# Sines of integer phases: contiguous reads, strided writes, and another order of multiples, sines and the upper half's sum

## The chip, the cores and the metric

The kernel runs on one core of a Trainium2 chip. The metric is the device time of one execution in microseconds (us), the median of several runs. The core's engines work in parallel, each through its own queue in program order: TensorE (PE, matmuls; PEld is its weight load), VectorE (DVE), ScalarE (ACT, activations), GpSimd (POOL) and SyncE (SP, which issues most DMAs). An instruction that waits holds back all that stand behind it in its engine's queue.

## The reference, cut to what matters

Two layers, each a state-space convolution and a gated feed-forward block, over 2048 tokens of 512 channels, in fp32:

```
x = x + ssm(layernorm(x));  x = x + ffn(layernorm(x))     # twice
ssm:  logdA = dt * (A_re + i A_im)          # 512 channels x 128 states
      P[d,n,l] = exp(logdA[d,n] * l)        # l = 0..2047
      K[d,l]   = Re sum_n C[d,n] P[d,n,l] dt B[d,n]
      y = causal convolution of u with K (by FFT) + u * Dskip
ffn:  (silu(x @ w_gate) * (x @ w_up)) @ w_down
```

The change lies in how the kernel makes K: for every channel and state it needs powers exp(logdA * l), whose phase is l * dt * A_im. The phase is kept as an integer, a fraction of a turn in 32 bits, so that a multiple of it is an integer sum that wraps around by itself.

## The kernel before, in words

The 128 states lie on the 128 partitions. The 512 channels are done in 8 chunks of 64 (DC = 64). A power l = 64 b + a is split into a table over a (`re`, `im`, 64 channels x 65 entries, made from exponentials, sines and cosines of multiples) and a table over b (`g`, made by doubling). For each chunk `lags` (L486) multiplies the two on TensorE, 128 small matmuls, into K; K goes by a copy (`spread_in`, L497) and DMAs into the order in which `spectra` (L534) transforms it.

The steps that the change and the prediction touch:

- `turn_units` (L362) turns dt * A_im into integers of a turn, `th` (one step) and `th32` (32 steps): two products on VectorE (L370), a conversion to integers on ScalarE (L371), a subtraction and two conversions on VectorE (L372, L374). Its scratch is `ft`. It runs for the channels 0 to 127 at the start, and for 128 to 255 and 256 to 511 later (L942, L951, L952).
- `gen_turns` (L376), VectorE: five small multiples for the doubling, into `xz` (L380), and sixteen multiples of `th32` into the scratch `tu` (L382, L386), which has the order partition, multiple m, channel d.
- `gen_trig` (L391), ScalarE, in three steps. First the small ones (L395 and one round of L399 to L401 on `xz`). Then for the lower half, m = 0 to 15: absolute value into `re` (L399), sine into `im` (L400), cosine in place in `re` (L401). Then the same for the upper half. `re` and `im` have the order channel, multiple, with 65 entries (260 bytes) per channel. L399 and L400 read `tu` through a transposed view, so they read at a stride of 256 bytes and write in runs of 16.
- `gen_upper` (L404), VectorE: adds the sixteenth multiple to all sixteen, in place in `tu` (L407). It must come after the lower half's sines have read `tu`, and before the upper half's.
- `gen_exp` (L409), ScalarE: five Exps into `mz`, twenty Exps into columns of `re` (L419), two squares (L431). `upper` (L423): a square into `mu` (L425).
- `gen_e` (L434) and `gen_g` (L451), VectorE: the products that finish `re` and `im` (L440 to L448) and the doubling of `g` (L455 to L483; `take(gg, n)` does n steps of it). The last doubling ends with a DMA that adds (L473).
- `gen_w` (L174), VectorE: the product of B, C and dt. `norm_early` (L278) normalizes the first 512 tokens; `direct` (L283) transforms them on TensorE (L289), and ScalarE copies the result out (L292).
- `norms` (L304) loads pieces of the feed-forward weights; ScalarE squares them (L323), TensorE sums the squares (L326), VectorE takes the largest (L329).

ScalarE holds one set of function tables at a time. Exp and Sin are in different sets, and a change of set is an instruction of its own, ACT_TABLE_LOAD. Copy, Square and Abs cause none in this kernel.

The order of work is written out by hand. Inside `tc.manual_schedule` (L936) ScalarE, VectorE and TensorE execute in the order in which the program issues. The start (L937 to L989) is a plain sequence. From the first `lags` on, the steps are put into `plan` by `at(time, step)` (L994), and the plan is sorted: its times only set the order. One turn of the plan begins with `lags` of chunk i, does `gen_e` and `gen_g` of chunk i + 1 and the multiples, sines and Exps of chunk i + 2, and the spectra of chunks i - 1 and i. Turns start 31 or 28 units apart. The places within a turn, by their plan times, as far as they matter here:

| plan time | step | engine |
|---|---|---|
| 0.0 | `lags` of chunk i | TensorE |
| 0.2 | `upper` of i + 1; `gg` steps until 12.2, two L440 at 0.3 and 2.3 | ScalarE; VectorE |
| 6.9, 17.5 | spectra of i - 1 and of i, L523 | TensorE |
| 7.1 | copy of `lags`' result, L499 | ScalarE |
| 8.0, 14.5 | squares of weights, first and second group, L323 | ScalarE |
| 12.6 | `gen_exp` of i + 2 | ScalarE |
| 13.9, 17.45 | sums of these squares, L326 | TensorE |
| 14.0, 17.6 | transform of later tokens, L289, and its copy, L292 | TensorE, ScalarE |
| 14.0, 17.3 | evacuation of the spectra, L550 and L551, L553 | ScalarE, VectorE |
| 14.4 to 16.0 | the five steps of `gen_turns` of i + 2 | VectorE |
| 17.4, 19.6, 21.8 | the three steps of `gen_trig` of i + 2 | ScalarE |
| 21.5 | `gen_upper` of i + 2 | VectorE |
| 22.0 | the rest of `gen_e` of i + 1: L443, L445, L448 | VectorE |

The last step of `gen_e`, L448, completes what the next `lags` reads.

Of the kernel before, what the change touches and what calls it, by code (L numbers as in the profile page):

```python
# [14 lines left out]
I32 = mybir.dt.int32  # L15
# [6 lines left out]
L, D, F = 2048, 512, 1376  # L22
P = 128
# [11 lines left out]
DC = 64  # L35
# [38 lines left out]
def kernel(ctx, tc, x, a_re, a_im, b_re, b_im, c_re, c_im, log_dt, d_skip,  # L74
# [12 lines left out]
    def tl(shape, name, tag, dt=F32):  # L87
        return sb.tile(shape, dt, name=name, tag=tag, bufs=BUFS[tag])
# [85 lines left out]
    def gen_w():  # L174

        wt = tl([P, 2, D], "wt", "bt")
        V.tensor_tensor(bw, bw, dt.unsqueeze(1).to_broadcast([P, 2, D]), OP.mult)
        V.tensor_tensor(w0, bw, cr.unsqueeze(1).to_broadcast([P, 2, D]), OP.mult)
        V.tensor_tensor(wt, bw[:, ::-1], ci.unsqueeze(1).to_broadcast([P, 2, D]), OP.mult)
        V.tensor_tensor(w0[:, 0], w0[:, 0], wt[:, 0], OP.subtract)  # L180
        V.tensor_tensor(w0[:, 1], w0[:, 1], wt[:, 1], OP.add)
# [13 lines left out]
    def stats(src, rows, scale, tag="stats", between=None, then=None):  # L195

        st = tl([P, 4, 6], "st", tag)
        mv = tl([P, 4, 2], "mv", tag)
        rs = tl([P, 8], "rs", tag)
        nb = rs[:, 4:]  # L200
        for r in range(rows):
            if between and r == 2:
                between()
            V.bn_stats(st[:, r], src[:, r])
            V.bn_aggr(mv[:, r], st[:, r])
        V.tensor_scalar(rs[:, :rows], mv[:, :rows, 1], EPS, 1.0 / scale ** 2, OP.add, OP.mult)
        G.tensor_tensor(rs[:, :rows], rs[:, :rows], mhalf[:, :rows], OP.pow)
        if then:
            then()
        V.scalar_tensor_tensor(nb[:, :rows], mv[:, :rows, 0], -1.0, rs[:, :rows], OP.mult, OP.mult)  # L210
        return rs, nb
# [66 lines left out]
    def norm_early(xt, n, factors):  # L278
        rs, nb = factors
        for c in range(4):  # L280
            V.tensor_scalar(n[:, c], xt[:, c], rs[:, c:c + 1], nb[:, c:c + 1], OP.mult, OP.add)
# [77 lines left out]
        return re, im, mu, xz, mz, tu  # L359


    def turn_units(c0, c1):  # L362


        n = c1 - c0
        cs = slice(c0, c1)
        ft = tl([P, 2, 2, n], "ft", "sg")
        fr, fk = ft[:, 0], ft[:, 1].bitcast(I32)
        for i, scale in enumerate((1.0, 32.0)):
            V.scalar_tensor_tensor(fr[:, i], th[:, cs], scale / (2.0 * math.pi), dt[:, cs], OP.mult, OP.mult)  # L370
        A.activation(fk, fr, AF.Copy)  # L371
        V.tensor_tensor(fr, fr, fk, OP.subtract)  # L372
        for i, o in enumerate((th, th32)):
            V.tensor_scalar(o[:, cs].bitcast(I32), fr[:, i], TURN, TURN / 2 - 128.0, OP.mult, OP.min)  # L374

    def gen_turns(ch, ts):  # L376

        re, im, mu, xz, mz, tu = ts
        cs = slice(ch * DC, (ch + 1) * DC)
        V.tensor_tensor(xz[:, 1].bitcast(I32), th[:, cs].bitcast(I32).unsqueeze(1).to_broadcast([P, 5, DC]),  # L380
                        am.unsqueeze(2).to_broadcast([P, 5, DC]), OP.logical_shift_left)
        V.tensor_tensor(tu[:, 0:2], th32[:, cs].bitcast(I32).unsqueeze(1).to_broadcast([P, 2, DC]),  # L382
                        am[:, 0:2].unsqueeze(2).to_broadcast([P, 2, DC]), OP.logical_shift_left)
        yield
        for n in (2, 4, 8):
            V.tensor_tensor(tu[:, n:2 * n], tu[:, 0:n], tu[:, n - 1:n].to_broadcast([P, n, DC]), OP.add)  # L386
            yield
        G.memset(im[:, :, 32], 0.0)
        yield

    def gen_trig(ts):  # L391


        re, im, mu, xz, mz, tu = ts
        A.activation(xz[:, 2], xz[:, 1].bitcast(I32), AF.Sin, scale=-TWO_PI / TURN)  # L395
        tv = tu.rearrange("p m d -> p d m")
        for c, s, turns in ((xz[:, 0], xz[:, 1], xz[:, 1].bitcast(I32)), (re[:, :, 33:49], im[:, :, 33:49], tv),
                            (re[:, :, 49:65], im[:, :, 49:65], tv)):
            A.activation(c, turns, AF.Abs)  # L399
            A.activation(s, turns, AF.Sin, scale=TWO_PI / TURN)  # L400
            A.activation(c, c, AF.Sin, scale=-TWO_PI / TURN, bias=hpi)  # L401
            yield

    def gen_upper(ts):  # L404

        tu = ts[5]
        V.tensor_tensor(tu, tu, tu[:, 15:16].to_broadcast([P, 16, DC]), OP.add)  # L407
# [207 lines left out]
    def take(it, n):  # L615
        for _ in range(n):
            next(it, None)
# [302 lines left out]
    ts = [None] * (NCH + 2)  # L920
# [15 lines left out]
    with tc.manual_schedule(engines={mybir.EngineType.Activation, mybir.EngineType.DVE, mybir.EngineType.PE}):  # L936
# [2 lines left out]

        def turns():  # L940
            V.tensor_tensor(rho, rho, dt, OP.mult)
            turn_units(0, P)  # L942
            take(ex, 14)
            take(gen_turns(0, ts[0]), 5)
        stats_x = stats(xe, 4, 1.0, between=turns)
        tr = gen_trig(ts[0])
        take(tr, 2)
        gen_upper(ts[0])
        take(tr, 1)
        take(ex, 11)  # L950
        turn_units(P, D // 2)  # L951
        turn_units(D // 2, D)  # L952
        gen_w()
        norm_early(xe, ne, stats_x)
        fw = [direct(0, h, q, [ne[:, c, h * HD:(h + 1) * HD] for c in range(4)]) for h in range(2) for q in QORD]
        for f in fw:
# [3 lines left out]
        gg = gen_g(0, ts[0], gs[0])  # L960
        ge, tn = gen_e(ts[0]), gen_turns(1, ts[1])
# [2 lines left out]
        upper(ts[0])  # L964
        take(fw[0], 1)
        take(fw[1], 1)
        stats_x = stats(x1, 4, 1.0)
        take(fw[2], 1)
        for g in (gg, ge, gg, ge, gg, ge, gg, ge, gg, tn, gg, tn, gg, tn, gg, tn, gg, tn):
            take(g, 1)  # L970
        tr = gen_trig(ts[1])
        take(tr, 2)
        gen_upper(ts[1])
        for c in range(4):
            A.activation(x1[:, c], x1[:, c], AF.Identity, scale=stats_x[0][:, c:c + 1], bias=stats_x[1][:, c:c + 1])
        take(fw[3], 1)
# [17 lines left out]
        def at(t, f, n=1):  # L994
            plan.append((t, len(plan), (lambda: take(f, n)) if hasattr(f, "__next__") else f))

        def later(make):

            yield from make()

        def prepare(c, t):

            def tiles():
                ts[c] = gen_tiles(c)
            at(t + 0.4, tiles)
            steps = {k: later(lambda g=g: g(c, ts[c])) for k, g in
                     (("turns", gen_turns), ("exp", gen_exp))}
            tr = later(lambda: gen_trig(ts[c]))
            for k in range(5):
                at(t + 14.4 + 0.4 * k, steps["turns"])  # L1010
            for k in range(3):
                at(t + 17.4 + 2.2 * k, tr)
            at(t + 21.5, lambda: gen_upper(ts[c]))
            at(t + 12.6, steps["exp"], 100)

        def factors(c, t):
# [59 lines left out]
        for i in range(NCH - 1):  # L1076
            t = starts[i]
# [5 lines left out]
            for k, t0, t1, t2, t3 in ((0, -1.4, 8.0, 13.9, 17.0), (1, 8.1, 14.5, 17.45, 19.5),  # L1083
                                      (2, 15.0, 26.5, 28.05, 36.0)):
                n = ((3, 3, 0), (3, 3, 0), (3, 3, 0), (3, 2, 0), (3, 2, 0), (3, 3, 0), (3, 3, 3))[i][k]
# [4 lines left out]
        t = starts[NCH - 1]  # L1090
# [8 lines left out]
        c, kts, tail = NCH - 1, (kt2[:, 0], kt2[:, 1]), {}  # L1099
# [148 lines left out]
```

## Time and profile before

| | us |
|---|---|
| median of three runs | 1213.85 (1213.76 to 1214.39) |
| the profiled execution, its own time | 1216.14 |
| span of the profiled execution | 1214.3 |
| PE busy | 1097.5 (90%) |
| DVE busy | 1007.3 (83%) |
| ACT busy | 623.5 (51%) |
| POOL busy | 92.8 (8%) |

How to read what follows. A line of the timeline has the start in us from the beginning of the span, the duration in us (of several merged instructions: from the first start to the last end), the engine, the line of the kernel, the operation, output <- input, partitions x elements with their types, and how many instructions are merged; in brackets the idle time of the engine just before, and what released it. A line of a group gives the number of instructions and their shortest, median and longest duration in ns, or busy us and mean ns. A line of the waits names who waited for whom, the total in us, how often, and the longest. A line of the stretches gives the window, its length, and the busy us of PE, PEld, DVE, ACT and POOL with their instruction counts, then the granted TensorE clock, the share of DMA and GB/s.

### The profile page before, as it was taken

The page shows a single profiled execution, that of the slowest core. Times are in us where ns is not written, and L with a number is a line of the kernel's source. Part 1 is how long each engine was busy: PE and PEld are TensorE (multiplying, and loading weights), DVE is VectorE, ACT ScalarE, POOL GpSimd, SP SyncE. Part 2 cuts the span into 40 slices and gives each one's busy share as a digit, 9 for nine tenths or more (in the row PEclk, how much of TensorE's full clock was granted, in tenths as well). Part 3 has the DMA queues.
Part 4 walks back from the last instruction along what each step waited for, and adds up shares of the span by engine and source line. Part 5 has one row for each costly group of instructions (what it writes and reads, how often), then busy time and mean ns, then how long its engine had stood idle before and what let it go on. Part 6 is the DMA issues. An engine that isn't in the chain of part 4 may idle for free.

```text
span 1214.3 us, 24571 instructions
## 1 busy us (share of the span) xinstructions
PE 1097.5 (90%) x10008; PEld 866.0 (71%) x10008; DVE 1007.3 (83%) x1612; ACT 623.5 (51%) x1205; POOL 92.8 (8%) x151
## 2 busy tenths in 40 slices
PE   0677888889989997999999999989999999999998
PEld 0555676767778684868687777858686776867875
DVE  3878888889879989899899999998997699984221
ACT  6398888993455255355745353564531553325111
POOL 1001111111000001001100000020100010000000
PEclk9988889889989999999999999999999999999999
DMA  5145665665748334732334444433435154312000
GB/s 207 44 149 129 144 142 151 152 174 165 256 140 260 118 117 144 183 116 92 86 113 141 124 157 129 133 102 116 124 120 152 60 133 132 117 57 45 14 23 18
DMA packets 136531, 151.17 MB, mean 124 GB/s; under 512 B 75473, under 2 KB 83665, under 8 KB 136418
## 3 DMA queue, kind: packets, MB, share of 16 engines
q1 hardware_dynamic: 129314, 126.47, 34.8%
q0 software_dynamic: 7104, 23.14, 7.3%
q8 instruction: 78, 1.28, 0.4%
q14 instruction: 35, 0.29, 0.1%
HBM read 101.85 MB, written 31.46 MB: 110 GB/s over the span
## 4 chain that ended last, share of the span: by engine, by line
PE 35%; DVE 27%; issue 4%; DMA 4%; ACT 2%; SPq 1%; POOL 0%; DVEq 0%; ACTq 0%; POOLq 0%
PE pgu L894 6%; PE pgu L895 6%; PE pgu L897 6%; DVE t L762 5%; DVE yk L765 4%; PE py L909 4%; PE py L910 4%; PE py L911 3%; PE pi L781 3%; PE pf L273 3%; DVE yk L762 2%; DMA mix<-nn 2%; DVE z L229 2%; DVE sg L901 2%; DVE bb L229 1%
## 5 line engine op out<-in xcount | busy, mean ns | idle before, releaser
L894 PE MATMUL pgu<-mix,wsl 128*128 128x256 f16 x1280 | 299.7, 273 | 5.3 <-DVE sg L901 2.7
L895 PE MATMUL pgu<-mix,wsl 128*128 128x256 f16 x1280 | 299.7, 273 | 0.0
L897 PE MATMUL pgu<-mix,wsl 128*128 128x256 f16 x1280 | 195.7, 273 | 0.0
L909 PE MATMUL py<-wsl,hh 128*128 128x512 f16 (+1 forms) x352 | 134.3, 381 | 8.8 <-DVE xg L914 7.1
L895 PEld LDWEIGHTS <-wsl 128*128 128x128 f16 x1280 | 125.5, 98 | 22.7 <-issue 6.5
L894 PEld LDWEIGHTS <-wsl 128*128 128x128 f16 x1280 | 125.3, 98 | 16.2
L897 PEld LDWEIGHTS <-wsl 128*128 128x128 f16 x1280 | 125.3, 98 | 15.0
L911 PE MATMUL py<-wsl,hl 128*128 128x512 f16 (+1 forms) x352 | 134.3, 382 | 0.3 <-DVE hl L903 0.3
L910 PE MATMUL py<-wsl,hh 128*128 128x512 f16 x320 | 122.0, 381 | 0.0
L762 DVE TENSOR_TENSOR t<-uu,w 128x1024 f32<-128x1024 f32 x96 | 117.7, 1226 | 2.7 <-DMA w<-wdr 2.5
L765 DVE TENSOR_TENSOR yk<-yk,t 128x1024 f32<-128x1024 f32 x96 | 117.7, 1226 | 0.3
L900 ACT ACTIVATE sg<-pgu,sc 128x512 f32<-128x512 f32 x80 | 54.6, 683 | 119.7 <-PE pgu L897 115.1
L901 DVE SCALAR_TENSOR_TENSOR sg<-pgu,sc,sg 128x512 f32<-128x512 f32 x80 | 60.3, 753 | 55.5 <-ACT sg L900 55.3
L523 PE MATMUL pw<-kt,ek 128*128 128x256 f32 (+1 forms) x384 | 93.6, 381 | 0.0
L902 ACT ACTIVATE hh<-sg 128x512 f16<-128x512 f32 x80 | 50.1, 626 | 77.2 <-DVE sg L901 77.1
L781 PE MATMUL pi<-yl,mix 128*128 128x256 f16 x576 | 78.9, 273 | 5.0 <-DVE yl L229 2.7
L493 PE MATMUL pk<-re,g 128*32 128x64 f32 x1024 | 46.2, 275 | 38.0 <-DVE re L448 33.1
L523 PEld LDWEIGHTS pw<-kt,ek 128*128 128x128 f32 x384 | 70.8, 194 | 8.3
L273 PE MATMUL pf<-z,eh 128*128 128x256 f16 x576 | 74.9, 273 | 0.0
L762 DVE TENSOR_TENSOR yk<-u,w0r 128x1024 f32<-128x1024 f32 x56 | 68.7, 1226 | 1.5 <-ACT u L275 1.5
L493 PEld LDWEIGHTS pk<-re,g 128*32 128x32 f32 x1024 | 41.0, 149 | 39.4 <-issue 39.4
L903 DVE TENSOR_TENSOR hl<-sg,hh 128x512 f16<-128x512 f32 x80 | 55.6, 696 | 15.4 <-ACT hh L902 15.3
(240 smaller groups left out, 2169.2 us busy)
## 6 DMA issues: line engine op xcount, KB each, us to landing
w<-wdr SPq DMA_DIRECT2D x96, 256.0 KB, 2.7
uu<-udr SPq DMA_DIRECT2D x96, 256.0 KB, 3.0
udr<-u POOLq DMA_DIRECT2D x32, 256.0 KB, 2.5
g<-acc POOLq DMA_DIRECT2D x6, 1024.0 KB, 9.0
udr<-u SPq DMA_DIRECT2D x16, 256.0 KB, 2.9
n<-ndr SPq DMA_DIRECT2D x16, 256.0 KB, 4.3
n<-xdr SPq DMA_DIRECT2D x4, 1024.0 KB, 5.7
kdr<-ks SPq DMA_DIRECT2D x6, 512.0 KB, 2.7
```

Source lines behind the costliest of these rows:

```text
L273: PE.matmul(pf[:, o], lhsT=e, rhs=m, start=k == 0, stop=k == len(terms) - 1)
L493: PE.matmul(o, lhsT=g[:, 0, :, d], rhs=re[:, d, 0:64], start=True, stop=False, tile_position=(0, 32 * grp))
L523: PE.matmul(pw[:, i], lhsT=e, rhs=kt[:, :, c + 4 * k0:4 * k1:4, :].rearrange("p g k d -> p k g d"), start=c == 0, stop=c == 3)
L762: V.tensor_tensor(t, uu.unsqueeze(1).to_broadcast([P, 2, 2, HD]), w.unsqueeze(2).to_broadcast([P, 2, 2, HD]), OP.mult)
L765: V.tensor_tensor(yk, yk, t, OP.add)
L781: PE.matmul(pi[:, o], lhsT=e, rhs=m, start=k == 0, stop=k == len(terms) - 1)
L894: PE.matmul(o, lhsT=wgu(wi, k, 0)[:, fs], rhs=nh[:, k], start=k == 0, stop=False)
L895: PE.matmul(o, lhsT=wgu(wi, k, 1)[:, fs], rhs=nh[:, k], start=False, stop=False)
L897: PE.matmul(o, lhsT=wgu(wi, k, 0)[:, fs], rhs=nlo[:, k], start=False, stop=k == 3)
L909: PE.matmul(py[:, r], lhsT=hh[:n, f, rc], rhs=wd(f, 0)[:n], start=f == 0, stop=False)
L910: PE.matmul(py[:, r], lhsT=hh[:n, f, rc], rhs=wd(f, 1)[:n], start=False, stop=False)
L911: PE.matmul(py[:, r], lhsT=hl[:n, f, rc], rhs=wd(f, 0)[:n], start=False, stop=f == FT - 1)
```

## The change

Four things are changed.

1. `gen_trig` turns the view around: the scratch `tu` is read in its own order, and the tables `re` and `im` are written through a transposed view, at a stride of 260 bytes. The cosine in place (L401) keeps its order.
2. `turn_units` becomes a generator of two steps over one shared scratch `ft` (in the buffers "ga" instead of "sg"), and runs for the channels 0 to 63 first and for all the others after that. The conversion on ScalarE of the others is issued before the first sines.
3. At the start `gen_w` and the second step for the other channels go ahead of `gen_upper` of chunk 0. The multiples of chunk 1 go ahead of the statistics of the next tokens, its first two steps of sines ahead of the products of chunk 0, and its `gen_upper` into the middle of them.
4. In each turn of the plan the multiples of chunk i + 2 move from 14.4 to 2.5, the first two steps of sines from 17.4 and 19.6 to 8.2, `gen_upper` from 21.5 to 13.0, and the third step of sines from 21.8 to 17.0. The Exps stay at 12.6.

```diff
-    def turn_units(c0, c1):
-        n = c1 - c0
+    def turn_units(ft, c0, c1):
         cs = slice(c0, c1)
-        ft = tl([P, 2, 2, n], "ft", "sg")
-        fr, fk = ft[:, 0], ft[:, 1].bitcast(I32)
+        fr, fk = ft[:, 0, :, cs], ft[:, 1, :, cs].bitcast(I32)
...
         A.activation(fk, fr, AF.Copy)
+        yield
         V.tensor_tensor(fr, fr, fk, OP.subtract)
...
+        yield
...
-        tv = tu.rearrange("p m d -> p d m")
-        for c, s, turns in ((xz[:, 0], xz[:, 1], xz[:, 1].bitcast(I32)), (re[:, :, 33:49], im[:, :, 33:49], tv),
-                            (re[:, :, 49:65], im[:, :, 49:65], tv)):
+        rows = [[t[:, :, 33 + m:49 + m].rearrange("p d m -> p m d") for t in (re, im)] for m in (0, 16)]
+        for c, s, turns in ((xz[:, 0], xz[:, 1], xz[:, 1].bitcast(I32)), (*rows[0], tu), (*rows[1], tu)):
             A.activation(c, turns, AF.Abs)
             A.activation(s, turns, AF.Sin, scale=TWO_PI / TURN)
+            c = c.rearrange("p m d -> p d m") if turns is tu else c
             A.activation(c, c, AF.Sin, scale=-TWO_PI / TURN, bias=hpi)
...
         def turns():
             V.tensor_tensor(rho, rho, dt, OP.mult)
-            turn_units(0, P)
+            take(first, 1)
             take(ex, 14)
+            take(others, 1)
+            take(first, 1)
             take(gen_turns(0, ts[0]), 5)
+        ft = tl([P, 2, 2, D], "ft", "ga")
+        first, others = turn_units(ft, 0, DC), turn_units(ft, DC, D)
...
         take(tr, 2)
+        take(others, 1)
+        gen_w()
         gen_upper(ts[0])
         take(tr, 1)
         take(ex, 11)
-        turn_units(P, D // 2)
-        turn_units(D // 2, D)
-        gen_w()
         norm_early(xe, ne, stats_x)
...
+        take(tn, 5)
         stats_x = stats(x1, 4, 1.0)
         take(fw[2], 1)
-        for g in (gg, ge, gg, ge, gg, ge, gg, ge, gg, tn, gg, tn, gg, tn, gg, tn, gg, tn):
-            take(g, 1)
         tr = gen_trig(ts[1])
         take(tr, 2)
+        for g in (gg, ge, gg, ge, gg, ge, gg, ge, gg, gg):
+            take(g, 1)
         gen_upper(ts[1])
+        take(gg, 3)
...
-            for k in range(5):
-                at(t + 14.4 + 0.4 * k, steps["turns"])
-            for k in range(3):
-                at(t + 17.4 + 2.2 * k, tr)
-            at(t + 21.5, lambda: gen_upper(ts[c]))
+            at(t + 2.5, steps["turns"], 5)
+            at(t + 8.2, tr, 2)
+            at(t + 13.0, lambda: gen_upper(ts[c]))
+            at(t + 17.0, tr)
             at(t + 12.6, steps["exp"], 100)
```

## The prediction

> **What bounds the kernel now.** The edits touch only the making of the tables of powers (L362 to L484), which the trace shows from 0 to about 300 us. So I read that part of the trace: first the waits of VectorE (DVE) and TensorE (PE) between 60 and 290 us, then the busy time by stretches, then the timeline of one chunk's turn on each engine. A wait's columns are: total us, times, longest.
>
> ```profile
> DVE tu L407 <- ACT im L400: 24.6, 7, 4.3
> PE pk L493 <- DVE re L448: 33.1, 6, 8.1
> 150.00:180.00 30.00, 25.00 (x341) 21.31 (x341) 25.70 (x30) 27.02 (x55) 4.53 (x7) 0.89 0.66 159
> ```
>
> VectorE stops seven times for 24.6 us before L407 (the upper half's sum). L407 overwrites the scratch `tu`, which ScalarE (ACT) must have read for the lower half's sines (L399, L400). TensorE waits 33.1 us for VectorE at the start of `lags`. Between 150 and 180 us PE, DVE and ACT are busy 25.0, 25.7 and 27.0 of 30 us: no engine has much room.
>
> ```profile
> 110.17 0.47 PE L493 MATMUL pk<-re,g 128*32 128x64 f32 x8 [8.08 <-DVE re L448]
> 142.03 0.47 PE L493 MATMUL pk<-re,g 128*32 128x64 f32 x8 [5.27 <-DVE re L448]
> 174.21 0.47 PE L493 MATMUL pk<-re,g 128*32 128x64 f32 x8 [5.00 <-DVE re L448]
> 269.83 0.47 PE L493 MATMUL pk<-re,g 128*32 128x64 f32 x8 [4.94 <-DVE re L448]
> ...
> 160.12 0.48 DVE L380 TENSOR_TENSOR xz<-th,am 128x320 int32<-128x320 int32 x1
> 162.23 0.95 DVE L553 TENSOR_TENSOR spare<-pw,spare 128x768 f32<-128x768 f32 x1
> 167.21 1.23 DVE L407 CUSTOM_DVE_ANT_0 tu<-tu 128x2048 uint16<-128x2048 uint16 x1 [4.03 <-ACT im L400]
> ```
>
> `lags` starts at 110.17 for chunk 1 and at 269.83 for chunk 6: 159.66 us for five turns, 31.93 each. In the turn that starts at 142.03 (32.18 us) TensorE has been idle for 5.00 us at its end, released by L448, and VectorE has idled 4.03 us before L407. Without that stop VectorE would need 28.15 us. So VectorE bounds the turn, and the stop is the prize.
>
> **The price of one strided activation.** L399 and L400 (16 each, 1024 elements) change from a strided read with a write in runs of 16 to a contiguous read with a write at a stride of 260 bytes. L401 keeps its pattern. The trace shows no such write at this length, so I bound it.
>
> ```profile
> L399 ACT ACTIVATE re<-tu x16: 1897/1970/2023, 18.2 to 264.1; 128x1024 f32<-128x1024 int32 x16
> L499 ACT ACTIVATE ks<-pk 128x1024 f32<-128x1024 f32 x8 | 8.2, 1021 | 25.0 <-PE pk L494 25.0
> L415 ACT ACTIVATE mz<-rho x40: 238/241/257, 13.0 to 248.5; 128x64 f32<-128x64 f32 x40
> L419 ACT ACTIVATE re<-rho x160: 298/304/322, 13.7 to 251.4; 128x64 f32<-128x64 f32 x160
> 152.99 3.08 ACT L419 ACTIVATE re<-rho 128x64 f32<-128x64 f32 x20
> L431 ACT ACTIVATE re<-re 128x512 f32<-128x512 f32 x8 | 9.1, 1141 | 0.0
> ```
>
> The strided read costs 1970 ns. A 1024-element activation that reads PSUM and writes without stride takes 1021 ns: the low end, a gain of 0.95 us each. L415 and L419 are the same 64-element Exp, contiguous and written at 260 bytes: 241 against 304 ns, 63 ns or 0.98 ns per element more. Over 1024 elements that is 1.02 + 1.01 = 2.03 us, against 1.97 now. L431 strides on both sides: (1141 - 600)/512, with 600 ns for a plain activation of 512 elements (the row at 53.44 below), is 1.06 ns per element, so 2.10 us: the high end. One row pleads for the low end: twenty L419 take 3.08 us, a pitch of 0.146 us, so the 63 ns overlap with the next one and could be a fixed latency. I take 1.97, **no change**, because L419 is the nearest row by its stride.
>
> [...]
>
> **The start, up to the first `lags`.**
>
> ```profile
> 19.13 0.16 DVE L210 SCALAR_TENSOR_TENSOR rs<-mv,rs 128x4 f32<-128x4 f32 x1 [1.23 <-POOL rs L207]
> 21.93 1.23 DVE L407 CUSTOM_DVE_ANT_0 tu<-tu 128x2048 uint16<-128x2048 uint16 x1 [2.64 <-ACT im L400]
> 23.19 1.93 ACT L399 ACTIVATE re<-tu 128x1024 f32<-128x1024 int32 x1 [0.20 <-DVE tu L407]
> 28.01 1.28 ACT L419 ACT_TABLE_LOAD   x1
> 31.36 0.42 DVE L372 TENSOR_TENSOR ft<-ft 128x256 f32<-128x256 f32 x1 [7.80 <-ACT ft L371]
> 33.74 0.69 DVE L372 TENSOR_TENSOR ft<-ft 128x512 f32<-128x512 f32 x1 [0.76 <-ACT ft L371]
> 34.88 1.22 DVE L177 TENSOR_TENSOR bw<-bw,dt 128x1024 f32<-128x1024 f32 x1
> 35.46 1.90 ACT L425 ACTIVATE mu<-re 128x1984 f32<-128x1984 f32 x1
> 39.73 1.91 DVE L281 TENSOR_SCALAR xne<-xne,rs 128x512 f32<-128x512 f32 x4
> 41.55 1.16 DVE L455 TENSOR_TENSOR xz<-xz,mz 128x960 f32<-128x960 f32 x1
> 53.44 0.60 ACT L292 ACTIVATE u<-pf 128x512 f32<-128x512 f32 x1 [2.86 <-PE pf L289]
> 54.38 0.49 DVE L380 TENSOR_TENSOR xz<-th,am 128x320 int32<-128x320 int32 x1
> 56.39 0.69 DVE L483 TENSOR_TENSOR g<-g,spare 128x512 f32<-128x512 f32 x1
> 60.20 1.23 DVE L483 TENSOR_TENSOR g<-g,spare 128x1024 f32<-128x1024 f32 x1
> 64.19 1.23 DVE L407 CUSTOM_DVE_ANT_0 tu<-tu 128x2048 uint16<-128x2048 uint16 x1 [2.77 <-ACT im L400]
> 75.79 0.36 PE L493 MATMUL pk<-re,g 128*32 128x64 f32 x7 [3.46 <-DVE g L483]
> ```
>
> Today VectorE waits 2.64 us at L407, then 7.80 us for a conversion (L371) that is queued on ScalarE behind all the sines and Exps; `gen_w` and the normalization (L281) stand behind it. After the change:
>
> 1. ScalarE converts the other 448 columns before the sines. From the plain activation of 512 elements (0.60 us), 896 elements take about 0.9 us, less 0.15 for the shorter first piece: the first sines come 0.75 later, and L400 ends at 21.93 + 0.75 = 22.7.
> 2. VectorE, free at 19.3 today, has some 0.5 us more before (products of 448 columns, less the shorter first piece): 19.8. Subtraction and two conversions: about 0.69 + 0.4 + 0.6, to 21.5. `gen_w`: 39.73 - 34.88 = 4.85, to 26.35. L407 then finds L400 long done, and ends at 27.5.
> 3. So L281 starts at 27.5, not 39.73: 12.2 us earlier, with the eight products of L289 behind it.
> 4. The upper sines take 28.01 - 23.19 = 4.82, to 32.4. L455 runs from 29.3 to 30.4; L459 waits until 32.5 for re[64], a new stop of some 2 us. ScalarE's work up to the end of L425 (35.46 + 1.90 = 37.36, 9.35 after 28.01) ends by 41.8 at the latest.
> 5. The third L292 comes with PE at 53.44 - 12.2 = 41.2 and ends at 41.85. Chunk 1's sines follow: load 1.28, small ones 1.70, L399 and L400 3.76 (durations from the turn below): 48.6. VectorE does what stood between 41.55 and 54.38 (12.83), the stop (2), the multiples that move forward (162.23 - 160.12 = 2.1) and two products of 512 (1.3): from 29.3 to 47.5. L407 starts at 48.6, not 64.19.
> 6. From L407 to `lags` today 75.79 - 64.19 = 11.6; three more steps of `gg` now come after it (0.69 + 3 x 1.23, less 0.2 of overlap): 15.8. First `lags` at 64.4: **11.4 us earlier**.
>
> **One turn in the steady part.** The turn from 142.03, on ScalarE and TensorE:
>
> ```profile
> 148.77 1.02 ACT L499 ACTIVATE ks<-pk 128x1024 f32<-128x1024 f32 x1 [3.61 <-PE pk L494]
> 159.96 1.28 ACT L395 ACT_TABLE_LOAD   x1
> 161.25 0.47 ACT L395 ACTIVATE xz<-xz 128x320 f32<-128x320 int32 x1
> 162.95 0.57 ACT L292 ACTIVATE u<-pf 128x512 f32<-128x512 f32 x1
> 163.42 1.91 ACT L399 ACTIVATE re<-tu 128x1024 f32<-128x1024 int32 x1
> 167.09 1.19 ACT L401 ACTIVATE re<-re,hpi 128x1024 f32<-128x1024 f32 x1
> 160.58 0.60 PE L326 MATMUL nrm<-sq,onesb 128*128 128x344 bf16 x3
> ```
>
> ScalarE copies `pk` at 148.77, T+6.74, when the 128 matmuls of `lags` are through. The second group of squares (L323) ends at 159.96, T+17.93, and the products of these squares start on TensorE at 160.58. Nothing waits there. After the change the plan puts two steps of sines (8.2) ahead of the Exps (12.6) and the squares (14.5). They take 162.95 - 161.25 = 1.70 and 167.09 + 1.19 - 163.42, less 0.09 of overlap, = 4.77: **6.47 us**. The squares end at T+24.40. Behind them on TensorE's queue stand L326 (17.45) and then the spectra (17.5), which need no squares, and then the next `lags`. From 160.58 TensorE needs 174.21 - 5.00 - 160.58 = 8.63 us, less some 0.2 because two of three products are done: next `lags` at T+32.8.
>
> VectorE loses its stop at L407 (ScalarE has read `tu` by T+15, L407 comes at about T+20) but waits for the evacuations before L553, at most until T+24.4; 0.95 and the 5.8 from the end of L407 (168.44) to 174.21 give T+31.2. So TensorE is late next, behind ScalarE's squares: 32.8 against 32.18, **0.6 us longer**, 3.1 in five turns. ScalarE's upper sines (1.28 + 4.8) end at T+30.5, in time for the next L459. The multiples (2.1 us) move within VectorE's queue, and hide. The larger `ft` in another buffer costs nothing: it is free at 21.5, long before `g` is written. SP's and POOL's queues lose and gain no transfer.
>
> The turn of chunk 0 (75.79 to 110.17, 34.4 us) has the same chain: one load of tables more (the Exps of chunk 1 come before the sines), no evacuations yet, longer squares. An estimate of 33.1, a gain of 1.3. The last turn before 300 us has no sines: unchanged.
>
> [...] Counted here, the steady turn keeps two loads, since its first sines find the previous turn's set; two are added in chunk 0's turn. [...]
>
> **Sum.** -11.4 - 1.3 + 3.1 = -9.6 us. What follows 300 us is unchanged and starts earlier. The profiled execution took 1216.14 (span 1214.3, 1.84 around it), so 1206.5 by its time; the median of three is 1213.85, 2.3 less: **1204.3**.
>
> **The rivals.** The chance of the forecast (1200 to 1208.5) is 0.58.
> - Strided writes run at full rate (1.02): 0.95 x 2 less on the chain, once in the start, once in chunk 0's turn, in five turns: 7 x 1.9 = 13.3, so 1191. For it: the pitch of L419. Against: its 304 ns. 0.20.
> - Slower than before: strided writes are dearer than strided reads. The place is the same, the lower half's two activations ahead of the squares. The gain is eaten at 9.6/14 = 0.69 us more each, 2.66 us; at 3.0 us it gives 1219. Against: L431's 2.10 with both sides strided. 0.09.
> - TensorE is not held by the squares: then ScalarE's own 28.6 us bound the turn (32.18 less the 3.61 of idle time before its copy at 148.77), 3.6 less instead of 0.6 more, 21 us in five turns: 1183. Against: L326 stood right before the spectra in every turn. 0.05.
> - The start gives half (the evacuations or Exps late): 1210. 0.08.
>
> **Range.** 1190 to 1211 takes in the forecast, the full rate and half of the last case: 0.82. A measurement of this kernel can tell about 0.2% (2.4 us) from no change. Faster by more: 0.58 + 0.20 + 0.05 + 0.04 = 0.87; within: 0.04; slower: 0.09.
>
> **What would show it.** L399 and L400 near 1.9 to 2.1 us (near 1.0: first rival). No wait of L407 for L400 in the turns; a new wait of L326 for L323 of about 6 us in each, `lags` every 32.8 us. L281 at about 27.5, first `lags` at about 64.4. Wrong would be a period below 30, or a first `lags` after 70.

## The result, and the profile after

| | before | after |
|---|---|---|
| median, us | 1214.12 (four runs, 1213.76 to 1215.66) | 1222.2 (four runs, 1221.13 to 1224.01) |
| the profiled execution, its own time | 1216.14 | 1224.01 |
| its span | 1214.3 | 1222.2 |

The changed kernel is slower: 1.0066 of the time before, interval 1.0048 to 1.0083. The forecast was 1204.3 with a range of 1190 to 1211. By the profiled executions the change was to bring -9.6 us and brought +7.9, so 17.5 us have to be found.

**First the page.** Its first part gives each engine's busy time, its share and its instructions. Before:

```profile
PE 1097.5 (90%) x10008; PEld 866.0 (71%) x10008; DVE 1007.3 (83%) x1612; ACT 623.5 (51%) x1205; POOL 92.8 (8%) x151
```

After:

```profile
PE 1110.8 (91%) x10008; PEld 867.2 (71%) x10008; DVE 1008.0 (82%) x1607; ACT 626.8 (51%) x1206; POOL 93.0 (8%) x151
```

VectorE works as long as before, ScalarE 3.3 us longer. TensorE has the same 10008 matmuls and is busy 13.3 us longer with them. No edit touches a matmul. This one pair of lines already says that the same matmuls run more slowly.

**Then the waits** between 50 and 290 us (who waited for whom: us, times, longest). TensorE:

```profile
PE nrm L326 <- ACT sq L323: 35.9, 7, 9.7
PE pk L493 <- DVE g L483: 6.3, 1, 6.3
```

VectorE:

```profile
DVE spare L553 <- ACT w0r L551: 15.9, 5, 3.8
DVE wo L553 <- ACT w0r L551: 12.9, 5, 5.5
DVE g L459 <- DMA g<-acc: 5.3, 3, 2.7
```

The wait of `lags` for L448 is gone (33.1 us before), and so is that of L407 for L400 in the turns. In their place TensorE waits 35.9 us for the squares before it sums them (L326), and VectorE waits for the evacuations of the spectra (L551), which ScalarE does late. The forecast had both, with their places. The 6.3 us for L483 are the wait of the first `lags`, at the end of the start; L459's wait for the adding DMA is a small new one.

**Then when each turn begins.** The first matmul of `lags`, from the timeline of TensorE:

```profile
64.62 0.47 PE L493 MATMUL pk<-re,g 128*32 128x64 f32 x8 [6.32 <-DVE g L483]
102.36 0.37 PE L493 MATMUL pk<-re,g 128*32 128x64 f32 x8
137.57 0.37 PE L493 MATMUL pk<-re,g 128*32 128x64 f32 x8
171.90 0.37 PE L493 MATMUL pk<-re,g 128*32 128x64 f32 x8
274.66 0.37 PE L493 MATMUL pk<-re,g 128*32 128x64 f32 x8
303.78 0.37 PE L493 MATMUL pk<-re,g 128*32 128x64 f32 x8
```

`lags` now starts without a wait, because TensorE is itself the late one. Inside it there is a new stop, which comes up below. The first one comes at 64.62 (forecast 64.4). Turn 0 lasts 37.74 us (forecast 33.1, before 34.38), the five turns from 102.36 to 274.66 last 172.30, or 34.46 each (forecast 32.8, before 31.93), and the last one 29.12 (before 28.89, from 269.83 to 298.72). What lies behind the last of these starts takes 1222.2 - 303.78 = 918.4 us, against 1214.3 - 298.72 = 915.6.

| where the 17.5 us are | forecast | measured | difference |
|---|---|---|---|
| start, up to the first `lags` | -11.4 | -11.2 | +0.2 |
| turn 0 | -1.3 | +3.4 | +4.7 |
| turns 1 to 5 | +3.1 | +12.6 | +9.5 |
| last turn | 0 | +0.2 | +0.2 |
| everything behind it, unchanged code | 0 | +2.8 | +2.8 |

The last row is within what the other kernels below show for that same code in their one profiled execution each (914.2 to 919.6), and I look no further into it. The rest lies in the turns.

**Last the stretch that is too long.** In the turn from 137.57 to 171.90 ScalarE and TensorE do this (start, duration, line, count, idle time and releaser):

```profile
143.31 1.02 ACT L499 ACTIVATE ks<-pk 128x1024 f32<-128x1024 f32 x1 [2.65 <-PE pk L494]
147.05 2.07 ACT L398 ACTIVATE re<-tu 128x1024 f32<-128x1024 int32 x1
159.61 1.27 ACT L323 ACTIVATE sq<-st 128x344 bf16<-128x344 f32 x3
160.18 1.20 PE L326 MATMUL nrm<-sq,onesb 128*128 128x344 bf16 x3 [4.85 <-ACT sq L323]
161.17 1.16 PE L523 MATMUL pw<-kt,ef 128*128 128x256 f32 x2
```

The squares end at 159.61 + 1.27 = 160.88, 17.57 behind the copy L499; the forecast had 24.40 - 6.74 = 17.66. The sines of the lower half, from L398 on, lie ahead of them. So ScalarE does what was foreseen. But from there to the next `lags` it takes 11.02 us, where the forecast had 32.8 - 24.4 = 8.4. Behind a wait of 4.85 us two matmuls L523 take 1.16 us. In the kernel before, where the same two stood behind other matmuls, they took 0.60. The stretches (window, length, busy us of PE, PEld, DVE, ACT and POOL with counts, then the granted TensorE clock) tell why. After:

```profile
126.60:131.00 4.40, 4.40 (x12) 3.16 (x11) 4.35 (x4) 4.37 (x3) 0.85 (x2) 0.50 0.77 182
131.00:137.50 6.50, 6.50 (x27) 5.05 (x25) 5.75 (x7) 3.15 (x5) 0.00 (x0) 0.89 0.49 135
160.00:165.60 5.60, 5.42 (x13) 3.39 (x13) 5.60 (x5) 5.57 (x6) 1.68 (x3) 0.50 0.91 200
165.60:172.00 6.40, 6.40 (x31) 5.02 (x33) 4.55 (x6) 3.12 (x5) 0.00 (x0) 0.93 0.48 136
```

Before, the same spectra in two windows and then the starts of two `lags`:

```profile
161.00:165.00 4.00, 4.00 (x20) 3.27 (x19) 2.11 (x4) 3.96 (x7) 2.43 (x4) 1.00 0.76 131
165.00:169.30 4.30, 4.20 (x19) 3.07 (x18) 2.09 (x2) 4.11 (x4) 0.00 (x0) 1.00 0.99 161
174.20:178.00 3.80, 3.79 (x144) 3.80 (x145) 3.80 (x6) 3.13 (x6) 0.00 (x0) 0.50 0.02 4
205.70:209.00 3.30, 3.23 (x122) 3.26 (x126) 3.30 (x5) 3.19 (x6) 0.00 (x0) 0.51 0.00 0
```

Behind its wait TensorE has half the clock, in the third of these windows for the whole 5.60 us: 12 matmuls of the spectra take 4.40 us, where the kernel before did 20 in 4.00. The spectra take from 161.17 to 171.90, 10.7 us, instead of 8.2 (174.21 - 5.00 - 161.02). The kernel before paid for its stop as well: its 5.00 us before `lags` at 174.21 are followed by a clock of 0.50. So are 4.99 us ahead of the one at 205.77 (0.51). There the slow stretch fell on the small matmuls of `lags`.

So the wait was not lengthened, it was moved from `lags` to the spectra, and `lags` should have gained by it. It did, but little: from its start to the copy L499 it took 6.74 us before and takes 143.31 - 137.57 = 5.74 now, at a full clock (1.00). That is not because a cold `lags`, one at half the clock, is cheap. Two stretches of the same length at the start of `lags`, both from the full filler below, one cold (0.50) and one warm (1.00):

```profile
63.24:66.54 3.30, 3.30 (x125) 3.30 (x129) 3.30 (x5) 3.27 (x4) 0.00 (x0) 0.50 0.61 204
199.34:202.64 3.30, 3.30 (x211) 3.30 (x214) 2.30 (x7) 2.98 (x4) 0.00 (x0) 1.00 0.91 268
```

In that warm turn the spectra's first matmul starts 4.20 us after `lags` (203.54 - 199.34). In the kernel after the copy came 0.16 us behind that matmul (143.31 - 143.15), so it comes here at about T+4.4, an estimate, 2.4 less than the 6.74 before. The kernel after gets only 1.0 of this, mostly because its warm `lags` stops in the middle, with no releaser in the trace ("issue"):

```profile
141.79 0.31 PE L493 MATMUL pk<-re,g 128*32 128x64 f32 x4 [1.04 <-issue]
```

Each of its turns 1 to 5 has such a stop, of 0.88 to 1.79 us, 5.8 us together; before there is one, of 0.79 us. **The half clock moved to the spectra, which lost 2.5 us by it, and `lags` gave back only 1.0.** What the stop in `lags` waits for no run here shows.

Six of the seven waits for the squares in the kernel after lasted 4.85 to 9.67 us, one in each of the turns 0 to 5. Behind every one of them the spectra started at a clock of 0.50, over their first 4.3 to 4.6 us.

### The profile page after: what moved, and what is told of

Same layout as the page of the kernel before. It is cut to its first block, busy times and chain, and to the rows that moved or that the text cites. A ratio compares the mean times of both kernels' runs of the same rounds, so it can differ in the third digit from the quotient of the medians.

```text
span 1222.2 us, 24563 instructions
## 1 busy us (share of the span) xinstructions
PE 1110.8 (91%) x10008; PEld 867.2 (71%) x10008; DVE 1008.0 (82%) x1607; ACT 626.8 (51%) x1206; POOL 93.0 (8%) x151
## 3 DMA queue, kind: packets, MB, share of 16 engines
q8 instruction: 78, 1.28, 0.4%
## 4 chain that ended last, share of the span: by engine, by line
DVE 30%; PE 29%; issue 6%; DMA 4%; ACT 1%; POOL 1%; SPq 1%; DVEq 0%; ACTq 0%; POOLq 0%
DVE t L762 5%; PE pgu L894 5%; PE pgu L895 5%; PE pgu L897 5%; DVE yk L765 4%; PE py L909 3%; PE py L910 3%; PE py L911 3%; DVE yk L762 3%; DVE z L229 3%; PE pi L781 2%; DMA mix<-nn 2%; PE pf L273 2%; DVE sg L901 2%; DVE hl L903 1%
## 5 line engine op out<-in xcount | busy, mean ns | idle before, releaser
L900 ACT ACTIVATE sg<-pgu,sc 128x512 f32<-128x512 f32 x80 | 54.7, 683 | 124.8 <-PE pgu L897 115.1
L523 PE MATMUL pw<-kt,ek 128*128 128x256 f32 (+1 forms) x384 | 103.8, 411 | 0.0
L523 PEld LDWEIGHTS pw<-kt,ek 128*128 128x128 f32 x384 | 77.4, 212 | 11.3
L910 PEld LDWEIGHTS <-hh 128*128 128x128 f16 (+1 forms) x352 | 34.8, 99 | 46.2 <-issue 11.5
L781 PEld LDWEIGHTS <-mix 128*128 128x128 f16 x576 | 56.0, 98 | 13.2 <-issue 3.7
```

What stands on the lines that cost most here:

```text
L523: PE.matmul(pw[:, i], lhsT=e, rhs=kt[:, :, c + 4 * k0:4 * k1:4, :].rearrange("p g k d -> p k g d"), start=c == 0, stop=c == 3)
L781: PE.matmul(pi[:, o], lhsT=e, rhs=m, start=k == 0, stop=k == len(terms) - 1)
L910: PE.matmul(py[:, r], lhsT=hh[:n, f, rc], rhs=wd(f, 1)[:n], start=False, stop=False)
```

## The experiments

The theory: the squares hold TensorE up, and the half clock behind that wait makes the spectra some 2.5 us longer in each turn. The rivals: the strided writes are to blame; or the start gives back what it gains; or VectorE's waits for the late evacuations set the turn, and TensorE's clock is a side show.

All ten stand beside runs of the kernel before on the same chip. "Turns 1 to 5" is the mean of five turns in the profiled execution, from one first matmul of `lags` to the next.

| kernel | median, us | ratio to before, interval | first `lags` | turn 0 | turns 1 to 5 |
|---|---|---|---|---|---|
| before | 1214.12 | | 75.79 | 34.38 | 31.93 |
| after | 1222.2 | 1.0066 (1.0048 to 1.0083) | 64.62 | 37.74 | 34.46 |
| strided reads again | 1221.04 | 1.006 (1.0045 to 1.0076) | 64.01 | 37.63 | 34.78 |
| new start, old places | 1202.13 | 0.9903 (0.9887 to 0.992) | 64.56 | 30.90 | 31.85 |
| old start, new places | 1235.62 | 1.0164 (1.0149 to 1.0179) | 76.21 | 38.22 | 34.66 |
| sums later | 1205.73 | 0.9932 (0.9915 to 0.9949) | 64.84 | 27.94 | 32.61 |
| sums later, GpSimd in order | 1193.09 | 0.9821 (0.9796 to 0.9845) | 64.15 | 28.00 | 30.26 |
| filler, first try | 1221.86 | 1.0061 (1.0041 to 1.0082) | 63.86 | 37.75 | 33.23 |
| filler, full | 1205.22 | 0.9908 (0.9887 to 0.9929) | 63.24 | 36.94 | 32.04 |
| squares early | 1196.63 | 0.9847 (0.9821 to 0.9873) | 65.42 | 28.98 | 31.47 |
| squares and evacuations early | 1189.72 | 0.9791 (0.9772 to 0.9809) | 64.05 | 30.44 | 29.30 |
| the same with strided reads | 1189.41 | 0.9785 (0.9764 to 0.9805) | 63.03 | 30.50 | 29.51 |

### The strided accesses

After, with the old read through the transposed view:

```diff
-        rows = [[t[:, :, 33 + m:49 + m].rearrange("p d m -> p m d") for t in (re, im)] for m in (0, 16)]
-        for c, s, turns in ((xz[:, 0], xz[:, 1], xz[:, 1].bitcast(I32)), (*rows[0], tu), (*rows[1], tu)):
+        tv = tu.rearrange("p m d -> p d m")
+        for c, s, turns in ((xz[:, 0], xz[:, 1], xz[:, 1].bitcast(I32)), (re[:, :, 33:49], im[:, :, 33:49], tv),
+                            (re[:, :, 49:65], im[:, :, 49:65], tv)):
```

> The changed kernel, but ScalarE reads the scratch through the transposed view again and writes runs of 16: order new, pattern old. Theory: each of the two activations falls from 2.08 to 1.97 us, 0.2 us per turn in front of the squares, 1220 to 1222 us. Rival A (the strided writes are the cause): 1208 to 1214 us.

1221.04: the loss stays. The group of L398 of the kernel after (L399 before; count, then shortest, median and longest ns), writing strided:

```profile
L398 ACT ACTIVATE re<-tu x16: 2033/2070/2104, 18.6 to 263.9; 128x1024 f32<-128x1024 int32 x16
```

The same activation in this kernel, reading strided:

```profile
L399 ACT ACTIVATE re<-tu x16: 1929/2008/2052, 18.5 to 263.3; 128x1024 f32<-128x1024 int32 x16
```

2070 against 2008 ns, and 1970 in the kernel before: it costs about the same on either side, and neither the first rival of the forecast (1.02 us) nor its slower one (from 2.66 us on) holds.

### The two halves of the change

After, with the steps at their old places in the turns:

```diff
-            at(t + 2.5, steps["turns"], 5)
-            at(t + 8.2, tr, 2)
-            at(t + 13.0, lambda: gen_upper(ts[c]))
-            at(t + 17.0, tr)
+            for k in range(5):
+                at(t + 14.4 + 0.4 * k, steps["turns"])
+            for k in range(3):
+                at(t + 17.4 + 2.2 * k, tr)
+            at(t + 21.5, lambda: gen_upper(ts[c]))
```

> The changed kernel with the old places in the turns (multiples 14.4 to 16.0, sines 17.4, 19.6, 21.8, upper half's sum 21.5): start and strided writes new. Theory (the start gains 11 us and keeps it, the turns lose): first lags at about 64.6, turns of about 32.2 us, 1201 to 1204 us. Rival (the start's gain is lost again in what follows it, by a cold clock or late transfers): 1209 us or more.

1202.13, as expected. The start keeps all it gains, and VectorE's old wait is back:

```profile
DVE tu L407 <- ACT im L399: 21.5, 6, 4.4
```

And the other half: the kernel before with the new places and the strided writes, and the old `turn_units` and start:

```diff
-            for k in range(5):
-                at(t + 14.4 + 0.4 * k, steps["turns"])
-            for k in range(3):
-                at(t + 17.4 + 2.2 * k, tr)
-            at(t + 21.5, lambda: gen_upper(ts[c]))
+            at(t + 2.5, steps["turns"], 5)
+            at(t + 8.2, tr, 2)
+            at(t + 13.0, lambda: gen_upper(ts[c]))
+            at(t + 17.0, tr)
```

> The kernel before with the new places in the turns and the strided writes, and the old start. Theory (start and turns add up; the turns alone cost 20 us, the start alone brings 12): 1231 to 1236 us. Rival (they do not add: the turns are slow only behind the early start): 1214 to 1224 us.

1235.62, as expected, 20.0 us above the 1215.63 of the kernel before beside it. So the start gives -12.0, the places +20.0, together +8.0, and measured is +8.1. By the medians the two halves add up; the loss is all in the places.

### TensorE kept busy, with the squares where they are

This is the run that separates the clock from the wait. After, with the transforms L289 that stand ahead of the waiting sums done several times over into the same place (the squares come no earlier). The first try doubles them:

```diff
-        for i in range(2):
+        for i in [0, 1] * (2 if b else 1):
             for c in range(4):
```

> The changed kernel, but each product of the later tokens (L289) in the turns is computed twice into the same place, so that TensorE works 3.4 us longer in front of the sums of squares; nothing is left out, the second pass overwrites the first. Theory: the wait for the squares shrinks from 4.9 to about 1.5 us in turns 1 to 5, the granted clock of the spectra behind it stays near 1 instead of 0.50, they take 8.2 instead of 10.7 us, and the turns fall from 34.4 to about 32: 1209 to 1213 us although there is more work. Rival (no clock in it: the spectra are slow because of their transfers or weight loads): the spectra still take 10.7 us, 1221 to 1224.

1221.86: missed, in the time and in the turns (33.23). The filler was too short. Two lines of TensorE's timeline:

```profile
123.43 1.19 PE L326 MATMUL nrm<-sq,onesb 128*128 128x512 bf16 x3 [1.78 <-ACT sq L323]
158.53 1.06 PE L326 MATMUL nrm<-sq,onesb 128*128 128x344 bf16 x3 [1.40 <-ACT sq L323]
```

Waits of 1.40 to 1.78 us are left in the five turns, and behind three of them (1.78, 1.43, 1.41) the clock was low all the same (0.51, 0.64 and 0.66 in the first 4.4 to 5.5 us; 1.00 behind the other two). It is ahead of the kernel after by 6.9 us where the last turn starts (267.75 against 274.66), and loses that in the last turn (36.4 us against 29.12). There no matmul waits for the squares, and the doubled transforms are plain extra work, 3.4 us. About as much, 3.3 us, is lost on the first spectra of that turn: they run cold (0.52 from 274.50 to 280.00) behind a stop of 2.21 us inside `lags`, again one for which the trace shows no releaser. The same stretches as above, at the first of these waits:

```profile
124.50:130.00 5.50, 5.50 (x14) 4.01 (x14) 5.50 (x5) 5.47 (x4) 0.85 (x2) 0.51 0.91 193
130.00:136.00 6.00, 6.00 (x26) 4.59 (x24) 4.46 (x6) 2.08 (x4) 0.00 (x0) 0.88 0.63 189
```

So the second try fills the wait to the end, and leaves out the turn that has none:

```diff
-        for i in range(2):
+        for i in order:
...
-            at(t - 3.0, lambda: box.append(second(*sec[k])))
+            at(t - 3.0, lambda: box.append(second(*sec[k], order=((0, 1, 0, 1, 0, 1, 0) if k == 0 else (0, 1, 0, 1, 0) if k < 6 else (0, 1)))))
```

> The changed kernel with TensorE kept busy through the whole wait: the products of the later tokens are repeated in the turns 0 to 5 only (2.5 times the work there, 3.5 times in turn 0; the last turn and the tail as they were), so that no wait for the squares is left. Nothing is left out. Theory (half clock after the wait): the spectra take 8.2 us at a clock of 1.0 in each of the turns 1 to 5 instead of 10.7, turns of 32.2 instead of 34.4, 1207 to 1211 us, with 29 us more TensorE work. Rival (the clock is not what counts, the squares alone do): the next lags come no earlier, 1221 to 1224 us.

1205.22, somewhat less than expected, and 17.0 us less than after, with 160 matmuls **more** (10168 against 10008; sixteen such matmuls take 3.45 us in the kernel before, from 157.13 to 160.58, so that 160 are some 34 us of work). Not all of the gain is the filler's. The profiled executions differ by 18.5 us: 12.1 lie in the turns 1 to 5, 0.8 in turn 0, 1.4 in the start and 4.2 behind the last turn, where the code is the same. The waits of TensorE for the squares, and the first half of the spectra in two turns:

```profile
PE nrm L326 <- ACT sq L323: 4.4, 2, 2.8
```

```profile
160.30:164.30 4.00, 4.00 (x20) 3.25 (x19) 4.00 (x4) 3.99 (x5) 0.00 (x0) 1.00 1.11 189
191.20:195.20 4.00, 4.00 (x20) 3.26 (x19) 4.00 (x4) 3.97 (x4) 0.00 (x0) 1.00 1.00 168
139.40:145.00 5.60, 5.60 (x16) 4.05 (x15) 5.43 (x10) 5.41 (x9) 1.93 (x5) 0.52 0.58 183
```

Twenty matmuls in 4.00 us at full clock, as in the kernel before. ScalarE's order is that of the kernel after, and in turn 0 its squares end as late as there: 18.83 us behind the copy L499 (88.67 - 69.84), in the kernel after 18.80 (90.06 - 71.26). In the turn from 168.41 to 199.34 the spectra start at T+22.81 instead of T+23.60 (this `lags` did not stop), and the turn ends at T+30.93 instead of T+34.33: 2.6 of these 3.4 us lie in the spectra. Over the turns 1 to 5 the spectra behind the squares take 41.3 us instead of 53.8, which is the whole gain of these turns. That separates the two: with ScalarE in the order of the kernel after and a clock of 1.00 in the spectra behind the squares, four of the five turns are shorter than the forecast's 32.8 us. It also answers the rival of the late evacuations: VectorE still waits for L551 in this run (12.0 us before L553 of `spare`, 15.9 in the kernel after), and the turns are short all the same.

The third line is from the turn that starts at 132.77, the one that is longer (35.64): its first spectra ran cold, behind a stop of 2.08 us in `lags` of the kind seen above. Turn 0 stays long (36.94): 2.75 us of its wait remained, and its spectra ran cold too (0.56 from 88.00 to 92.00).

### The wait taken away

The sums of the second squares can stand later, behind the spectra, or the squares earlier, ahead of the Exps. First the sums (after, with two other places; the fourth number is that of the sums' largest, L329):

```diff
-            for k, t0, t1, t2, t3 in ((0, -1.4, 8.0, 13.9, 17.0), (1, 8.1, 14.5, 17.45, 19.5),
+            for k, t0, t1, t2, t3 in ((0, -1.4, 8.0, 13.9, 17.0), (1, 8.1, 14.5, 17.6, 26.0),
```

> The changed kernel, but the second group's sums of squares (L326) stand behind the spectra on TensorE's queue (17.6 instead of 17.45), and their largest value is taken at 26.0. Theory (TensorE is held by the squares, and then runs its spectra at half clock): the waits of L326 for L323 (35.9 us) go nearly all, the granted clock in the spectra is back near 1, the turns fall from 34.4 to about 29.3 us (VectorE's evacuation and ScalarE's own work bound them), and the time to 1190 to 1200 us. Rival A (the dearer strided writes make it slow): nothing moves, 1221 to 1223. Rival B (ScalarE's order bounds the turn whatever stands on TensorE): the wait goes, but the turns stay at 33 to 34 us, 1217 to 1222.

1205.73, with turns of 32.61 us: missed. The wait for the squares is nearly gone (1.9 us), but another has come. TensorE's waits between 55 and 300 us:

```profile
PE pk L493 <- DMA g<-acc: 19.6, 4, 6.5
```

and GpSimd's queue in the turn from 128.47:

```profile
153.10 1.60 POOL L317 DMA_DIRECT2D st<-in_B_w_gate_dram  x3 [13.82 <-ACT sq L323]
154.69 1.27 POOL L473 DMA_DIRECT2D g<-acc  x1
```

The adding DMA of the last doubling (L473) has its input ready at 146.9 (L472, 144.62 + 2.28), but is issued behind weight loads (L317), whose buffers come free with the squares. The next `lags` waits for it. So I made the queue follow the program's order:

```diff
-        with tc.manual_schedule(engines={mybir.EngineType.SP}):
+        with tc.manual_schedule(engines={mybir.EngineType.SP, mybir.EngineType.Pool}):
```

> The kernel with the sums behind the spectra, and GpSimd's queue kept in the order of the plan as well. In the run without this, the adding DMA (L473) stood behind weight loads that waited for the squares, and lags waited 19.6 us for it. Theory: that wait goes, turns 1 to 5 fall to about 30 us, 1191 to 1197 us. Rival (the DMA's own landing time of 8 to 9 us bounds the turn): 1203 to 1207 us as without it.

1193.09, 12.6 less, and turns of 30.26 us, as expected; the DMA is issued at 145.06, ahead of the loads, and the wait has shrunk:

```profile
PE pk L493 <- DMA g<-acc: 12.9, 4, 3.9
```

Then the squares themselves, ahead of the Exps:

```diff
-            for k, t0, t1, t2, t3 in ((0, -1.4, 8.0, 13.9, 17.0), (1, 8.1, 14.5, 17.45, 19.5),
+            for k, t0, t1, t2, t3 in ((0, -1.4, 8.0, 13.9, 17.0), (1, 8.1, 12.3, 17.45, 19.5),
```

> The changed kernel with one number changed: the second group's squares go from 14.5 to 12.3, behind the first two steps of sines but ahead of the Exps. Theory (the squares hold TensorE): no wait of L326 for L323, spectra at full clock; VectorE still waits for the evacuations (L551) some 3 us, so turns of about 30 us: 1191 to 1197 us. Rival (other late things, such as the adding DMA, bound the turn): 33 us or more per turn, 1205 us or more.

1196.63, in the range, though the turns are longer than expected (31.47): one number moved, 25.6 us less than after. TensorE's stop is back before `lags` and VectorE's evacuations are next:

```profile
PE pk L493 <- DVE re L448: 16.1, 4, 4.3
```

```profile
DVE spare L553 <- ACT w0r L551: 12.8, 5, 3.7
```

So the evacuation of the first spectra in the turn was moved ahead of the Exps as well:

```diff
-                                      (n + 6.9, n + 14.0, n + 17.3, n + 22.0))))[:2 if c < NCH - 2 else 1]:
+                                      (n + 6.9, n + 12.4, n + 17.3, n + 22.0))))[:2 if c < NCH - 2 else 1]:
```

> As the kernel with the early squares, and the evacuation of the spectra (L550, L551) goes from 14.0 to 12.4, also ahead of the Exps. Theory: VectorE's wait for L551 goes too, turns of 28.5 to 29 us, bounded by VectorE's and ScalarE's own work: 1185 to 1192 us. Rival (the landing of the adding DMA or ScalarE's length bounds it already): the same as with the early squares alone.

1189.72, 0.9791 of the time before, as expected (the turns, 29.30, are a little longer): the change as a whole with its two victims moved out of the way beats both kernels, that of before by 25.9 us (1215.63 beside it) and that of after by 32.5. The same spectra there:

```profile
141.65:145.65 4.00, 4.00 (x20) 3.25 (x19) 4.00 (x4) 4.00 (x26) 1.20 (x1) 1.00 0.04 15
145.65:150.00 4.35, 4.18 (x19) 3.06 (x17) 4.35 (x4) 4.30 (x4) 0.03 (x1) 1.00 0.94 166
```

And this kernel with the strided reads in place of the strided writes, by the edit shown first:

> The kernel with the early squares and evacuations, but ScalarE reads the scratch through the transposed view and writes runs of 16, as before the change. Theory (a strided write is 0.1 us dearer than a strided read of the same 1024 elements, 0.4 us per turn of ScalarE's work): the same or up to 3 us less, 1187 to 1190 us. Rival (the pattern matters where ScalarE bounds the turn): 1180 us or less.

1189.41: no difference that can be told, in a kernel where TensorE waits for the squares in turn 0 only. No run here shows a gain from the first of the four edits by itself.

## Why the prediction was wrong

**The step that failed** is the sentence "From 160.58 TensorE needs 174.21 - 5.00 - 160.58 = 8.63 us, less some 0.2 because two of three products are done: next `lags` at T+32.8." The 8.63 us were read off a stretch in which TensorE came from other matmuls, at a granted clock of 1.00. The forecast itself put a wait of about 6 us in front of that stretch, and kept the duration. Measured are 11.02 us, 2.6 more in that turn and 2.65 in the mean of the turns 1 to 5, 13.3 us together. The forecast also kept the cold duration of `lags` (6.74 us to the copy L499). That was the other end of the same slip: with the wait gone from ahead of it `lags` ran warm, and could have given back some 2 us a turn (the copy comes at T+6.47 in the mean of the turns 1 to 5 before, and at about T+4.4, by the estimate above, in a warm turn of the full filler). It gave back 0.6 (T+5.85), mostly because of its own stops. The two together are 10.2 us in five turns, and the five turns missed by 9.5. That the spectra's part is the clock and not the wait is what the full filler shows.

In turn 0, 4.7 us over, the forecast's 33.1 has no working beside it. Its own terms give about 34: 17.8 for the end of the second squares before (93.57 - 75.79), 6.5 for the sines, 1.3 for the load and 8.4 behind. The squares did end there (T+25.44), and the spectra took 11.9 us (clock 0.50, then 0.78) instead of 8.2. No run here gave these spectra a warm clock with the squares where they are.

The trace of before had it in plain sight: a clock of 0.50 at the start of two of the `lags`, behind stops of 5.00 and 4.99 us. The forecast looked at what the stop said of VectorE and not at what it did to the next matmuls.

Point by point:

- **What bounds the kernel**: right as to the waits. "VectorE bounds the turn, and the stop is the prize" was half of it; the prize was real, as the last version shows with 29.30 us per turn, but ScalarE's order gave it away.
- **The strided activation**: right in the main. 1.97 us was taken, 2.07 and 2.10 measured, at the upper one of the bounds of 1.02 and 2.10.
- **The start**: right, from L281 at 26.92 (27.5) to the first `lags` at 64.62 (64.4).
- **ScalarE's order in the turn**: right. 6.47 us of sines ahead of the squares; copy to end of squares 17.57 against 17.66.
- **VectorE**: right that L407 no longer waits and L553 does, and that TensorE is later.
- **The tables**: right. 19 loads against 17, each 1.28 us, as counted. Both traces show one wherever ScalarE goes from Exps to sines or back, and besides these one at its first activation (a Copy, L171) and one at L900.
- **The rivals**: none was the true one. The slower one had the right sign and the wrong mechanism. A rival "the wait is in front of the spectra and costs them their clock" at the sizes measured, 9.5 + 4.7 us on top of 1204.3, would have given 1218.5; it was not among them.

What stays open: why waits of 1.4 to 1.8 us in the first filler cost the clock in three turns and not in two, and what `lags` stops for when it runs warm (0.88 to 1.79 us in the kernel after, 2.21 and 2.08 in one turn of each filler). The 2.8 us behind the last turn were not studied.

## What to carry to other kernels

When an edit puts a wait in front of a stretch of matmuls, do not price that stretch with its warm duration: look in the trace at the granted clock behind the stops that are already there, and take cold durations for what follows the new wait. And do not count on the stretch that the wait has left: here it gave back 0.6 us a turn of the 2 or so estimated from a warm turn of the full filler. When one engine's order is changed, list who waits for each thing that is pushed back, not only for the thing that is pulled forward; here a group of squares and an evacuation, each moved by about two units in the plan, turned +8 us into -26. And an addition of two halves tells quickly whether a loss comes from a meeting or from one of them.

## What was not expected of the hardware

- The half clock cost small and large matmuls nearly alike: 125 instead of 211 of the 64-column ones of `lags` in 3.30 us, 12 in 4.40 us instead of 20 in 4.00 of the 256-column fp32 ones of the spectra. It lasted 3.4 to 5.6 us behind the stops ahead of `lags` in the kernel before, and 5.7 to 6.8 us behind the waits for the squares in the turns 1 to 5 of the kernel after (9.3 in turn 0), read in windows of 0.25 us.
- A `lags` at full clock stopped inside for some 1 us with no releaser in the trace, in each of the turns 1 to 5 of the kernel after (0.88 to 1.79 us); in the kernel before, where it starts at 0.50, in one of the five (0.79 us).
- Stops shorter than the 4.85 to 9.67 us of the kernel after were followed by a low clock too: in the turns 1 to 5 of the first filler waits of 1.41, 1.43 and 1.78 us (0.66, 0.64 and 0.51), but not those of 1.40 and 1.44 us (1.00); in the full filler stops of 2.08 and 2.75 us (0.52 and 0.56). The length alone does not tell: behind the stop of 1.79 us inside a `lags` of the kernel after the clock stayed at 1.00.
- Useless matmuls paid: with 160 more, some 34 us of work, the turns 1 to 5 were 12.1 us shorter together, since the matmuls ran where TensorE would have stood still.
- The ScalarE activations that read 1024 elements of `tu` took 2.07 and 2.10 us with strided writes (medians of L398 and L399 in the kernel after), 2.01 and 2.00 with strided reads in their place (L399 and L400 of that run), and 1.97 and 1.96 in the kernel before, against 1042 ns for L593 of the kernel before, which strides nowhere (and reads fp32, not integers). The copy L499 took 1021 ns in the kernel before, though it reads PSUM through a transposed view, at a stride of 256 bytes.
